# A planned attention and MLP kernel: instruction fetches in the planner's DMA model, and other splits of layer 1 in stripes 2 and 4

## The chip, the cores and the metric

The kernel runs on one core of a Trainium2 chip. The core has a matrix engine (PE, or TensorE), a vector engine (DVE), a scalar engine (ACT), a general engine (POOL, or GpSimd), and a synchronisation engine (SP) whose work here is to issue transfers. Sixteen DMA engines move data between HBM and the on-chip memory. Each engine works through its own instructions in order and waits on semaphores for the others. The metric is the device time of one execution in microseconds (us), lower is better. Durations of single instructions are in us or ns as the profile gives them.

## The reference

Two computations follow one another. The first is a decayed linear attention over 4 batches, 8 heads, 768 positions and head dimension 64, in blocks; the second is a two-layer MLP over the 3072 tokens that come out of it, with a piecewise quadratic activation.

```python
for b in range(nb):                      # blocks of 64 positions
    intra = einsum('bhic,bhjc->bhij', qb, kb) * Dmask
    intra = einsum('bhij,bhjd->bhid', intra, vb)
    inter = einsum('bhid,bhde->bhie', qb * lam_pow, kv_state)
    out[:, :, sl] = intra + inter
    kv_state = lam_block * kv_state + einsum('bhsd,bhse->bhde', kb_dec, vb)
x = out.transpose(0, 2, 1, 3).reshape(3072, 512)
h = x @ w_in                             # 512 -> 2048
g = where(h >= 1, h, where(h <= -1, 0, (h + 1) ** 2 / 4))
y = g @ w_out                            # 2048 -> 512
```

## The kernel before

The tokens are cut into 24 **chunks** of 128, six to a batch, and into six **stripes** of 512 tokens (four chunks each, stripes 0 to 5). Chunk c belongs to stripe c // 4.

*Attention, per chunk.* SP loads k and v of a chunk (256 KB each), and q for two chunks at a time (512 KB). GpSimd scales and casts q (line 249) and k (line 243; VectorE does k of the first four chunks). ScalarE casts v (line 263). From chunk 6 on, k and q are transposed by transfers that SP issues (lines 289 and 292); before that PE transposes them (lines 268 and 275). PE updates the running state ("u", line 298), which ScalarE copies out (line 302). PE forms the scores ("s", line 317 from chunk 4 on), VectorE masks them ("m", line 327), PE forms the chunk's output ("o", lines 334 and 337), and ScalarE casts that into the stripe's transposed activations xT ("x", line 344).

*MLP, per stripe.* Layer 1 is 16 steps, each of which fills one PSUM bank of 128 x 512 with h (line 365). With `PARTS[s] = n`, the stripe is cut into n parts of 512/n tokens: a step then computes n groups of 128 hidden features for one part, by 4n matmuls of 512/n columns, and a part's steps need only that part's chunks. Without an entry n is 1. ScalarE takes r = relu(h + 1) out of the bank (line 373). Two steps make one VectorE group: t (line 381), w (384) and gT (389). Layer 2 is 16 steps of four matmuls of 512 columns (line 408), four steps to each output tile of 128 tokens; ScalarE copies that out (line 413) and SP stores it (line 430). A layer-2 step of a stripe in several parts needs the groups of its part; in a stripe with n = 1 it needs the groups of its quarter of the features. PE works on layer 1 of stripe s and layer 2 of stripe s - 1 in turn, with attention of later chunks in between. The steps of layer 1 are counted through all stripes (16 for each, "step 32" is the first of stripe 2), and so are the groups (8 for each), the output tiles and their stores (4 for each).

*The order.* All of this is laid out ahead of time by a planner, `run_plan` (line 179), which runs while the program is built. `add` (line 175) registers an operation with its engine, an assumed duration, what it needs, and a due time. The planner simulates the engines with these assumed durations, and whenever an engine is free it takes, among the operations that are ready by then, the one with the earliest due time. It sends out the instructions of every engine in the order of the simulated start times. Transfers go through one modelled queue, `dma_free`: a transfer starts when the queue is free and occupies it for its `dma` time. On the chip each engine then keeps to this order, whatever arrives late.

Due times come from a ladder, `l_seq` (line 435): one step of `STEP` for each layer-1 and layer-2 step. An attention chunk is due (`o_due`, line 451) 3 us ahead of the first layer-1 step of the part that it belongs to, and chunks of the same part are 3 us apart. The transposes of q and k are due first of all on SP, then loads in their order, then stores.

Buffers also tie things together: six loads of k and of v and three of q may be in flight or unused, four cast k tiles, two banks for h, two for y, three VectorE groups, and eight output tiles that wait to be stored.

Of the kernel before, what the change touches and what calls it, by code (L numbers as in the profile page):

```python
# [23 lines left out]
def kernel(  # L24
# [24 lines left out]
    KO = d_model // 128  # L49
# [7 lines left out]
    LQ, NQ2 = 3, 3  # L57
# [4 lines left out]
    XT, NQT, NQK, RING = 6, 4, 4, 3  # L62
# [112 lines left out]
    def add(key, eng, ns, fn, needs=(), due=None, extra=0, dma=0, perf=False):  # L175
        OPS[key] = Op(key, eng, ns, fn, needs, due, extra, dma, perf)
        ops.append(OPS[key])

    def run_plan(free):

        users = {x.key: [] for x in ops}
        for x in ops:
            x.needs = [OPS[y] for y in x.keys if y in OPS]
            for y in x.needs:
                users[y.key].append(x)
        left = {x.key: len(x.needs) for x in ops}
        topo = [x for x in ops if not x.needs]
        for x in topo:
            for u in users[x.key]:
                left[u.key] -= 1  # L190
                if left[u.key] == 0:
                    topo.append(u)
        assert len(topo) == len(ops)
        for x in reversed(topo):
            d = [u.due - u.ns - x.extra - LAT for u in users[x.key] if not u.dma]
            x.due = min(d + ([x.own] if x.own is not None else []), default=1e9)
            if x.dma or x.key[0] in ("l1", "l2"):
                x.due = x.own
        left = {x.key: len(x.needs) for x in ops}
        ready = {e: [] for e in free}  # L200
        for x in topo:
            if not x.needs:
                ready[x.eng].append((0, x))
        out_seq, xfer, dma_free = [], [0] * RING, 0
        while len(out_seq) < len(ops):
            t, e = min((max(free[e], min(r for r, _ in lst), xfer[-RING] if e == "SP" else 0), e)
                       for e, lst in ready.items() if lst)
            r, x = min(((r, x) for r, x in ready[e] if r <= t), key=lambda p: (p[1].due, p[0]))
            ready[e].remove((r, x))
            ns = x.ns + (720 if x.perf and free["POOL"] > t else 0)  # L210
            free[e] = t + ns
            x.t, x.end = t, t + ns + x.extra
            if x.dma:
                dma_free = max(dma_free, t + (1300 if e == "SP" else 2100)) + x.dma
                x.end = dma_free + 1400
                if x.key[0] in ("ld", "lq") and x.key[1] >= (FAR if x.key[0] == "ld" else FAR // 2):
                    x.end += SLACK if (x.key[1] if x.key[0] == "ld" else 2 * x.key[1]) >= 10 else NEAR
                if e == "SP":
                    xfer.append(dma_free)
            out_seq.append((t, len(out_seq), x))  # L220
            for u in users[x.key]:
                left[u.key] -= 1
                if left[u.key] == 0:
                    ready[u.eng].append((max(y.t if y.eng == u.eng and y.key != u.gate else y.end + (XSL if u.eng == "SP" and y.eng == "POOL" and u.dma in (640, 1280) else LAT) for y in u.needs), u))
        for t, _, x in sorted(out_seq, key=lambda p: p[:2]):
            if DBG:
                print(f"{t / 1e3:9.3f} {x.due / 1e3:9.3f} {x.eng:5s} {x.ns:6.0f} {x.key}")
            x.fn()

    def mm(*cols):  # L230
        return sum(c / 2.4 + 3 for c in cols)


    qs, ks, kT, qT, sc_sb, xT, ptt, pst, pot = {}, {}, {}, {}, {}, {}, {}, {}, {}
# [56 lines left out]
    def f_qx(m):  # L291
        nc.sync.dma_start_transpose(out=qT_tile(m).rearrange("p e h j -> p (e h) j"), in_=qs[m].rearrange("p e h d -> p (e h d)"))
# [138 lines left out]


    T0, STEP, LEAD = 22000, 1057, 3000
    PARTS = {1: 4, 2: 4, 3: 2, 4: 2}
    l_seq = [(1, 0, i, 0) for i in range(FO)]
    for s in range(1, NST + 1):
        n = PARTS.get(s, 1)
        l1 = [(1, s, i, p) for p in range(n) for i in range(0, FO, n)]
# [44 lines left out]
    for it in order:  # L483
        if isinstance(it, tuple):
# [4 lines left out]
            if gated is not None:  # L489
                need.append(("w",) + w_seen[gated])  # L490
            add(("w",) + it, "POOL", 900, lambda it=it, wait=gated: f_w(it, wait), need, due=pos_ * 1e-3,
                dma=2560)
# [17 lines left out]
    for c in range(NCH):  # L510
        od, cb = o_due(c), c % NCB
        lastu = c - 1 if cb else c - 2
        m = c // 2
        e = "DVE" if c < CPS else "POOL"
        add(("cast", c, 1), e, 690 if e == "DVE" else 1060, lambda c=c, eng=(nc.vector if e == "DVE" else nc.gpsimd): cast(c, eng),
            [("ld", c, 1), ("cast", c - 1, 1), ("t", c - NQK), ("u", c - NQK)])
        add(("cast", c, 2), "ACT", 640, lambda c=c: cast_v(c),
            [("ld", c, 2), ("o", c - NV), ("u", c - NV), ("cast", c - 1, 2)])
        for i in range(2 if c % 2 == 0 else 0):
            old = ("tq", m - NQK // 2, i)  # L520
            add(("cq", m, i), "POOL", 1060, lambda m=m, i=i: cast_q(m, i, nc.gpsimd),
                [("lq", m), ("cq", m, 0) if i else None, old, ("qT",) + old[1:]])
            if m < XQ:
                add(("tq", m, i), "PE", mm(*[128] * 4), lambda m=m, i=i: f_tq(m, i),
                    [("cq", m, i)] + ([("kT", c - 1), ("m", c - 1, 1), ("tq", m, 0) if i else None] if c >= CPS else []),
                    due=od - 6000, extra=FILL)
                add(("qT", m, i), "ACT", 600, lambda m=m, i=i: f_qT(m, i), [("tq", m, i)])
            else:
                if i:
                    add(("qT", m, 1), "SP", 2000, lambda m=m: f_qx(m), [("cq", m, 1), ("o", 2 * (m - NQ2) + 1)], due=-2, dma=1280)  # L530
        if c < XT:
            add(("t", c), "PE", mm(*[128] * 4), lambda c=c: f_t(c),
                [("cast", c, 1), ("kT", c - 1), ("kb", c - 1, 0), ("kb", c - 1, 1), ("m", c - 1, 1) if c > 3 else None,
                 ("qT", m, 0) if c >= CPS and c % 2 == 0 and m < XQ else None, ("qT", m, 1) if c >= CPS and c % 2 == 0 and m < XQ else None],
                due=od - 6000, extra=FILL)
        else:
            add(("t", c), "SP", 1200, lambda c=c: f_kx(c), [("cast", c, 1), ("m", c - NQT, 1)], due=-2, dma=640)
        if CPS <= c < XT:
            add(("kT", c), "DVE", 450, lambda c=c: f_kT(c), [("t", c), ("m", c - NQT, 1)])
        for hi in range(2 if c < CPS else 0):  # L540
            add(("kb", c, hi), "DVE", 365, lambda c=c, hi=hi: f_kb(c, hi), [("t", c), ("s", c - NKB, 1)])
        if cb < NCB - 1:
            add(("u", c), "PE", mm(*[128] * 4), lambda c=c: f_u(c),
                [("cast", c, 1), ("cast", c, 2), ("ub", lastu, 0), ("ub", lastu, 1), ("u", lastu)], due=od - 4000, extra=FILL)
            for hi in range(2):
                add(("ub", c, hi), "ACT", 372, lambda c=c, hi=hi: f_ub(c, hi), [("u", c), ("o", c - NUB + 1)])
        if c >= CPS:
            add(("s", c, 0), "PE", mm(*[128] * 4) + 190, lambda c=c: f_s2(c),
                [("kT", c) if c < XT else ("t", c), ("qT", m, 0), ("qT", m, 1), ("m", c - 1, 0), ("m", c - 1, 1)], due=od - 2500, extra=FILL)
        for h in range(2):  # L550
            if c < CPS:
                add(("s", c, h), "PE", mm(*[128] * 4), lambda c=c, h=h: f_s(c, h),
                    [("kb", c, 0), ("kb", c, 1), ("qT", m, 0), ("qT", m, 1), ("m", c - 1, 0) if not h else ("t", c)], due=od - 3000 + 100 * h, extra=FILL)
            add(("m", c, h), "DVE", 690, lambda c=c, h=h: f_m(c, h), [("s", c, h if c < CPS else 0), ("o", c - 3), ("m", c, 0) if h else None])
        add(("o", c), "PE", mm(*[128] * (12 if cb else 8)), lambda c=c: f_o(c),
            [("m", c, 1), ("cast", c, 2), ("ub", c - 1, 0) if cb else None, ("ub", c - 1, 1) if cb else None,
             ("x", c - 1), ("o", c - 1)], due=od, extra=FILL)
        add(("x", c), "ACT", 600, lambda c=c: f_x(c), [("o", c), ("x", c - 1), ("l1", (c // CPS - 2) * FO - 1)])


    n1, last = 0, None
    l1_order = [x for x in l_seq if x[0] == 1]
    l2_order = [x for x in l_seq if x[0] == 2]
    NA = 4
# [4 lines left out]
    for n1, (_, s, i, p) in enumerate(l1_order):  # L569
# [2 lines left out]
        rw = RW  # L572
        j = (i // n) % rw
        grp = n1 // rw
        add(("l1", n1), "PE", mm(*[MS // n] * (KO * n)) if n1 >= NA else mm(*[C] * KO),
            lambda a=(s, i, n, p, 1 if n1 < NA else None): f_l1(*a),
            kx + [("w", 0, W_OF[i + n - 1]), ("la", n1) if n1 < NA else ("r", n1 - 2 if n1 >= NA + 2 else n1 - NA), ("l1", n1 - 1)], due=l_due[1, s, i, p], extra=FILL)
# [57 lines left out]
```

## Time and profile before

| what | us |
|---|---|
| median of 8 runs | 225.23 |
| lowest and highest of the 8 | 224.16, 228.63 |
| the profiled execution | 224.22 |
| its span, first to last instruction | 222.5 |
| layer 1 on PE (line 365), busy | 93.6 |
| layer 2 on PE (line 408), busy | 87.7 |
| VectorE, the three operations of a group, mean ns | 576, 806, 832 |
| ReLU on ScalarE, mean ns | 679 |
| VectorE idle ahead of its first group operation, waiting for the ReLU | 41.0 |
| GpSimd waiting for q loads, for k loads | 30.8, 17.6 |
| k transposed by a transfer, issue to landing, median (range) | 2.9 (2.4 to 5.3) |
| q transposed by a transfer, issue to landing, median (range) | 5.2 (3.3 to 6.7) |
| v load, issue to landing, median (range) | 5.4 (3.4 to 8.4) |

The granted TensorE clock was full in every slice of the span. In a row of the timeline the first number is the start in us from the start of the span, the second the length, then engine, line, operation, output and inputs, shape and count; what stands in brackets is how long the engine had stood idle before and what released it. PE overlaps the matmuls of a row, and the recorded length of one (219 ns for 128 columns) is longer than the distance to the next, so distances are taken from start to start. Some 30 matmul records are missing from the trace.

### The profile page before, as it was taken

What the parts mean: (1) busy time and instruction counts of PE and PEld (TensorE: products, weight loads), DVE (VectorE), ACT (ScalarE), POOL (GpSimd) and SP (SyncE); (2) the same over time, 40 slices, a digit from 0 to 9 for tenths busy, and PEclk for the clock granted to TensorE, in tenths of its full rate; (3) what the DMA queues carried; (4) which work ended last, traced back from release to release, by engine and by line L of the source; (5) the groups of instructions that cost most, each with busy time, mean ns of one, the idle gap of its engine ahead of it and who ended that gap; (6) DMA issues with size and microseconds to landing.
All of it is one profiled execution on the core that took longest, in us unless ns stands there. A gap on an engine that the chain in (4) does not pass through costs nothing. (4 is left out here: it accounts for less than half of the span.)

```text
span 222.5 us, 4630 instructions
## 1 busy us (share of the span) xinstructions
PE 204.2 (92%) x1874; PEld 135.2 (61%) x1904; DVE 144.2 (65%) x218; ACT 123.7 (56%) x221; POOL 64.6 (29%) x65
## 2 busy tenths in 40 slices
PE   0589897998999999999999989999999999999994
PEld 0376534776569787777667757767767644444442
DVE  4586496799656896989499458774556554654301
ACT  3475866546646866665665475767555445445030
POOL 7371074226625161918042065620000000000000
PEclk9999999999999999999999999999999999999999
DMA  5999999999997999979898999994011001110122
GB/s 130 240 201 199 188 242 200 183 227 216 172 259 150 191 200 203 170 173 185 197 183 313 239 216 270 194 210 98 2 47 50 20 27 50 47 47 0 47 97 94
DMA packets 89685, 34.39 MB, mean 155 GB/s; under 512 B 70080, under 2 KB 86720, under 8 KB 89664
## 3 DMA queue, kind: packets, MB, share of 16 engines
q1 hardware_dynamic: 85296, 29.89, 66.9%
q0 software_dynamic: 4224, 4.19, 11.9%
q8 instruction: 15, 0.25, 0.5%
q14 instruction: 6, 0.05, 0.1%
q10 hardware_dynamic: 144, 0.00, 0.0%
HBM read 27.27 MB, written 6.29 MB: 151 GB/s over the span
## 5 line engine op out<-in xcount | busy, mean ns | idle before, releaser
L365 PE MATMUL ph<-xT,w_in_sb 128*128 128x128 bf16 (+2 forms) x877 | 93.6, 255 | 0.9 <-ACT r L373 0.7
L373 ACT ACTIVATE r<-ph,one 128x512 bf16<-128x512 f32 (+2 forms) x96 | 64.6, 679 | 51.0 <-PE ph L365 35.6
L408 PE MATMUL py<-w_out_sb,gT 128*128 128x512 bf16 x341 | 87.7, 379 | 1.7 <-issue 0.5
L365 PEld LDWEIGHTS <-w_in_sb 128*128 128x128 bf16 x880 | 65.4, 98 | 24.3 <-issue 2.2
L381 DVE TENSOR_SCALAR t<-r 128x1024 bf16<-128x1024 bf16 x48 | 27.6, 576 | 41.0 <-ACT r L373 41.0
L408 PEld LDWEIGHTS <-gT 128*128 128x128 bf16 x368 | 33.9, 98 | 31.4
L389 DVE TENSOR_TENSOR gT<-w,t 128x1024 bf16<-128x1024 bf16 x48 | 39.9, 832 | 1.6
L249 POOL TENSOR_TENSOR qs<-x0f,tab_q 128x512 bf16<-128x512 f32 x24 | 28.8, 1220 | 38.3 <-DMA x0f<-in_q_dram 30.8
L384 DVE TENSOR_TENSOR w<-r,t 128x1024 bf16<-128x1024 bf16 x48 | 38.7, 806 | 1.3
L243 POOL TENSOR_TENSOR ks<-x1f,tab_k 128x512 bf16<-128x512 f32 x20 | 25.8, 1294 | 29.6 <-DMA x1f<-in_k_dram 17.6
L413 ACT COPY osb<-py 128x512 f32<-128x512 f32 x23 | 13.5, 586 | 14.4 <-PE py L408 12.7
L263 ACT CAST vi<-x2f 128x512 bf16<-128x512 f32 x24 | 14.9, 620 | 11.0 <-DMA x2f<-in_v_dram 10.9
L327 DVE TENSOR_TENSOR sc<-ps,causal 128x512 bf16<-128x512 f32 x20 | 13.8, 690 | 10.8 <-PE pt L317 10.8
L337 PE MATMUL po<-sc,vi 128*128 128x128 bf16 x192 | 18.2, 219 | 0.0
L344 ACT CAST xT<-po 128x512 bf16<-128x512 f32 x24 | 14.1, 588 | 6.8 <-PE po L337 3.0
L302 ACT CAST ubd<-pu 64x256 bf16<-64x256 f32 x40 | 14.6, 366 | 4.9 <-PE pu L298 4.5
L337 PEld LDWEIGHTS <-vi 128*128 128x128 bf16 x192 | 14.4, 98 | 2.7 <-issue 0.7
L334 PE MATMUL po<-qT,ubd 128*128 128x128 bf16 x80 | 14.5, 219 | 0.6 <-ACT xT L344 0.6
L327 DVE TENSOR_TENSOR sc<-pt,causal 128x512 bf16<-128x512 f32 x20 | 13.6, 681 | 0.0
L298 PE MATMUL pu<-vi,ks 128*128 128x128 bf16 x80 | 8.2, 228 | 1.8 <-POOL ks L243 1.1
L268 PE MATMUL pt<-ident,ks 128*128 128x128 bf16 x24 | 2.8, 249 | 7.3 <-DVE ks L243 7.2
L298 PEld LDWEIGHTS <-ks 128*128 128x128 bf16 x80 | 6.1, 102 | 4.5 <-POOL ks L243 2.2
(55 smaller groups left out, 89.0 us busy)
## 6 DMA issues: line engine op xcount, KB each, us to landing
x1f<-in_k_dram SPq DMA_DIRECT2D x24, 256.0 KB, 5.4
x0f<-in_q_dram SPq DMA_DIRECT2D x12, 512.0 KB, 5.6
x2f<-in_v_dram SPq DMA_DIRECT2D x24, 256.0 KB, 5.4
out_dram<-osb SPq DMA_DIRECT2D x23, 256.0 KB, 2.5
w_in_sb<-in_moe_w_in_dram POOLq DMA_DIRECT2D x4, 512.0 KB, 9.1
w_out_sb<-in_moe_w_out_dram POOLq DMA_DIRECT2D x4, 512.0 KB, 8.4
kT<-ks SPq DMA_TRANSPOSE x18, 2.9
out_dram<-osb SPq DMA_DIRECT2D x1, 192.0 KB, 1.9
```

The lines of the kernel that those rows point to most:

```text
L243: eng.tensor_tensor(ks[c], qkv_ld[c, 1], _bc(tab_k[:, c % NCB, :], 2, D), op=AX.mult)
L249: eng.tensor_tensor(qs[m, e], qkv_ld[m, 0][:, :, e], _bc(tab_q[:, e, m % (NCB // 2), :], 2, D), op=AX.mult)
L263: nc.scalar.copy(out=v_out(vi[c % NV]), in_=qkv_ld[c, 2].rearrange("p (a b) d -> p a b d", b=2))
L302: nc.scalar.copy(out=ubd[c % NUB][HD[hi], :, HD[hi]], in_=pu[0][HD[hi], :, HD[hi]])
L327: nc.vector.tensor_tensor(sc_sb[c][:, g], pst[c, g], _bc(causal, 1, HP), op=AX.mult)
L337: nc.tensor.matmul(po[:, hp], lhsT=vi[c % NV][:, hp, hi].rearrange("p a d -> p (a d)"), rhs=sc_sb[c][:, hi, hp, :], start=(cb == 0 and hi ...
L365: nc.tensor.matmul(ph[:, j * m:(j + 1) * m], lhsT=w_in_sb[:, ko, (ni + j) * 128:(ni + j + 1) * 128], rhs=xT[s][:, ko, part * m:(part + 1) ...
L373: nc.scalar.activation(out=r_t[grp][:, i, cs], in_=ph_t[s, ni, part][:, cs], func=AF.Relu, bias=one[:, 0:1])
L381: nc.vector.tensor_scalar(t_t[grp], r, 0.5, 1.0, op0=AX.mult, op1=AX.min)
L384: nc.vector.tensor_tensor(w_t[grp], r, t_t[grp], op=AX.subtract)
L389: nc.vector.tensor_tensor(gT[s][:, f - RW * n:f, part * m:(part + 1) * m], w_t[grp].rearrange("p a (b m) -> p (a b) m", m=m), t_t[grp].rea ...
L408: nc.tensor.matmul(py_t[s, ms], lhsT=gT[s][:, ko, ms * 128:(ms + 1) * 128], rhs=w_out_sb[:, ko, :], start=(ko == 0), stop=(ko == FO - 1))
```

## The change

There are three edits. First, the planner gets a model of PE's own instruction fetches. Every PE operation counts two instructions (a weight load and a matmul) for each of its matmuls: 8 matmuls for scores, 12 for a chunk's output, the layer-1 step's own number, 4 for everything else. Whenever the count passes a multiple of 256, the modelled DMA queue is taken for 1300 ns from that time on. Second, the assumed SP time of a q transpose goes from 2000 to 2450 ns. Third, stripe 2 is cut in two parts in place of four, and stripe 4 is left whole in place of two parts. No other line of the kernel is changed; the instructions of all operations but layer 1 of these two stripes stay as they were, and their order comes out of the planner.

```diff
+    MMS, FETCH = {"s": 8, "o": 12}, 1300
...
-        out_seq, xfer, dma_free = [], [0] * RING, 0
+        out_seq, xfer, dma_free, fetched = [], [0] * RING, 0, 0
...
             free[e] = t + ns
             x.t, x.end = t, t + ns + x.extra
+            if e == "PE":
+                n = fetched + 2 * MMS.get(x.key, MMS.get(x.key[0], 4))
+                if n // 256 > fetched // 256:
+                    dma_free = max(dma_free, t) + FETCH
+                fetched = n
             if x.dma:
                 dma_free = max(dma_free, t + (1300 if e == "SP" else 2100)) + x.dma
...
-    PARTS = {1: 4, 2: 4, 3: 2, 4: 2}
+    PARTS = {1: 4, 2: 2, 3: 2, 4: 1}
...
-                    add(("qT", m, 1), "SP", 2000, lambda m=m: f_qx(m), [("cq", m, 1), ("o", 2 * (m - NQ2) + 1)], due=-2, dma=1280)
+                    add(("qT", m, 1), "SP", 2450, lambda m=m: f_qx(m), [("cq", m, 1), ("o", 2 * (m - NQ2) + 1)], due=-2, dma=1280)
...
+        MMS["l1", n1] = KO * n if n1 >= NA else KO
         add(("l1", n1), "PE", mm(*[MS // n] * (KO * n)) if n1 >= NA else mm(*[C] * KO),
```

## The prediction

> **What bounds the kernel now.** I read the page first, for the engine that sets the end.
>
> ```profile
> span 222.5 us, 4630 instructions
> ...
> PE 204.2 (92%) x1874; PEld 135.2 (61%) x1904; DVE 144.2 (65%) x218; ACT 123.7 (56%) x221; POOL 64.6 (29%) x65
> ...
> DMA  5999999999997999979898999994011001110122
> ...
> q8 instruction: 15, 0.25, 0.5%
> ...
> PE 37%; DMA 2%; issue 1%; POOL 0%; DVE 0%; POOLq 0%
> ```
>
> TensorE is busy in 204.2 of 222.5 us, and the chain that ended last is nearly all PE, with one DMA in it. The DMA engines are full until about 145 us: attention loads decide when PE's attention pieces can run. All the change can win is PE's standing time and its pace; so I went through PE's timeline from matmul start to matmul start. From 7 to 25 us some 7 us are lost waiting on the prologue, whose order the change leaves alone. After 25 us PE really stands at four places, about 4 us together (a hole of 0.22 us beside a "x3" or "x7" of 512 columns is one missing record, not a wait):
>
> ```profile
> 34.39 0.40 PE L298 MATMUL pu<-vi,ks 128*128 128x128 bf16 x4 [1.05 <-POOL ks L243]
> ...
> 52.20 0.62 ACT L263 CAST vi<-x2f 128x512 bf16<-128x512 f32 x1 [2.79 <-DMA x2f<-in_v_dram]
> ...
> 52.87 0.38 PE L298 MATMUL pu<-vi,ks 128*128 128x128 bf16 x4 [0.57 <-ACT vi L263]
> ...
> 53.45 0.72 PE L365 MATMUL ph<-xT,w_in_sb 128*128 128x128 bf16 x10 [0.20 <-ACT r L373]
> ...
> 128.61 0.62 ACT L263 CAST vi<-x2f 128x512 bf16<-128x512 f32 x1 [2.39 <-DMA x2f<-in_v_dram]
> ...
> 129.87 1.03 PE L365 MATMUL ph<-xT,w_in_sb 128*128 128x256 bf16 x8 [0.52 <-ACT r L373]
> ...
> 144.17 3.63 DMA kT<-ks
> 147.80 0.05 issue
> ```
>
> Each time PE's fixed order asks for a chunk whose load, cast or transpose has not arrived. At 52 and 129 us ScalarE, itself in order, stands on a v load, and the ReLU that frees PE's bank is queued behind that cast.
>
> **The change, part by part.** The planner's new terms (a fetch charge, 2450 instead of 2000 for the q transpose) put no instruction into the program; they reorder it. The built program has 192 matmuls and 192 weight loads fewer, SP and POOL have the same instructions, and POOL the same order.
>
> *Pace.* Stripe 2 goes from 256 matmuls of 128 columns to 128 of 256, stripe 4 from 128 of 256 to 64 of 512. Starts of one 16-, one 8- and one 4-matmul step against the next:
>
> ```profile
> 89.58 1.06 PE L365 MATMUL ph<-xT,w_in_sb 128*128 128x128 bf16 x16
> 90.47 1.03 PE L408 MATMUL py<-w_out_sb,gT 128*128 128x512 bf16 x4
> 91.33 1.06 PE L365 MATMUL ph<-xT,w_in_sb 128*128 128x128 bf16 x16
> ...
> 112.63 1.04 PE L365 MATMUL ph<-xT,w_in_sb 128*128 128x256 bf16 x8
> 113.50 1.03 PE L408 MATMUL py<-w_out_sb,gT 128*128 128x512 bf16 x4
> ```
>
> A step of the same work takes 0.89, 0.87 and 0.86 us: 16 x 0.02 = 0.32 for stripe 2 and 16 x 0.01 (0.87 to 0.862 unrounded, 0.13) for stripe 4, **0.45 us** won. The Trainium skill, "TensorE: Matmul & The Clock Gate", Back-to-back issue gap, would make this the main thing: it gives about 81 ns sustained for a matmul of 128 columns with its weight load and 131 ns for 512 (98 ns for 256, by my interpolation). By that rule stripe 2 saves 256 x 81 - 128 x 98 = 8.2 us and stripe 4 128 x 98 - 64 x 131 = 4.2 us, an estimate of 12 us. The rows show 56, 109 and 216 ns at full granted clock, so weight loads are hidden already: I take 0.45.
>
> *The fetch charge.* The plan now stops its one model of the DMA queue for 1.3 us at every 256 PE instructions. The q8 row holds 15 fetches and 0.5% of 16 engines' span: 0.005 x 222.5 x 16 / 15 = 1.2 us each, but on one engine of 16. The skill ("Runtime: NRT & Kernel Launch", Instruction fetch mechanics) also says that crossing such a block is mostly hidden, which speaks against paying for it; in this trace no PE wait ends on one. By the rule the term is worth nothing; by the row it makes the plan up to 1.3 us too pessimistic about loads after each fetch. Its effect is only that attention is placed later behind its loads, which is what the waits above want.
>
> *Chunks 4 to 6.* PE's order was layer-1 step 10, q transpose, step 11, q transpose, then chunk 4; now one more step stands ahead of each transpose pair and of chunk 4's state update, 1.7 us of work. PE reaches that update at 34.5; its k cast ended at 34.34. The 1.2 us hole (33.12 to 34.39) and 0.3 us ahead of the transposes go; chunk 4's transpose then waits some 0.1 for ScalarE's copy out of its bank: **-1.4**. Chunk 6's update moves behind three more layer-2 steps (2.6 us): PE comes to it at about 53.3, its cast is done at 52.8. The holes there, 0.74 and 0.36 us, go; chunk 7's update may wait 0.1: **-1.0**.
>
> *Chunks 6 to 13.* Now I set PE's new turns (old starts, plus the steps moved ahead, less what was won) against landings. Chunk 6: turn 60.8, its transposes landed at 58.8 and 59.3 before and now sit ahead of a v load. Chunk 8: 73.1 against 70.4. Chunk 9: 76.9 against 75.8, now ahead of a v load. Chunk 10: 84.4; before, q and k landed at 85.2 and 85.9, but now they are issued ahead of both loads of chunk 13 (1.2 us of transfer each), so about 83.2: **the least slack, 1.2 us**. Chunk 11: 89.0 against some 86.4. Chunks 12 and 13: 3 us and more. Nothing added; the loads pushed back (v of chunk 8, k and v of 13, 15) are wanted by casts more than 3 us later.
>
> *Stripe 2 in halves.* Its first eight layer-1 steps now run with no layer-2 step between them. Two steps take PE 1.74 us and make one VectorE group, which takes 1.8 us alone and 4.1 us beside a GpSimd op:
>
> ```profile
> 37.44 0.42 DVE L381 TENSOR_SCALAR t<-r 128x1024 bf16<-128x1024 bf16 x1
> 37.89 0.69 DVE L384 TENSOR_TENSOR w<-r,t 128x1024 bf16<-128x1024 bf16 x1
> 38.62 0.69 DVE L389 TENSOR_TENSOR gT<-w,t 128x1024 bf16<-128x1024 bf16 x1
> ...
> 88.91 1.26 DVE L381 TENSOR_SCALAR t<-r 128x1024 bf16<-128x1024 bf16 x1
> 90.21 1.41 DVE L384 TENSOR_TENSOR w<-r,t 128x1024 bf16<-128x1024 bf16 x1
> 91.66 1.42 DVE L389 TENSOR_TENSOR gT<-w,t 128x1024 bf16<-128x1024 bf16 x1
> ```
>
> VectorE's order is chunk 10's mask, group 16, the first op of group 17, chunk 11's mask. The mask of 10 ends at about 86.3. With every op fast that of 11 ends by 90.1, before PE asks at 91.2; with every op slow (4.1 + 1.3 + 1.3) at 93.0, 1.8 late. GpSimd casts there about three quarters of the time, so not all are slow: I take **+0.65**, between 0 and 1.8. Behind it in PE's queue stand the chunk's output, xT and the second half. The first layer-2 step of stripe 2 now wants group 19 instead of 17: at about 105, against 99 to 106; 0, at most 1.3.
>
> *Chunks 16 to 23, stripe 4 whole.* Chunk 19's v cast moves on ScalarE from behind ReLU 55 to behind 61, some 8 us later than its load: the 0.69 us at 129 goes. All of chunk 19 must now precede stripe 4's first step. On SP, stores 9 and 10 move ahead of loads: store 9 (its copy ready near 122) ahead of chunk 19's, store 10 (near 131) ahead of those of 21 and 22 and of the k transpose of 19. From there I keep the old spacing (k load of 21 issued 130.3, transpose landed 142.0): it lands by 143.6, and PE asks at 146.4. Chunk 20's transposes wait on SP for store 11 (141) and land at 147; PE asks at 150.4 instead of 147.3: the 0.53 us goes. The eight steps of stripe 4 without layer 2 meet a GpSimd that is nearly done, so groups take 1.8 and cost nothing. From layer-1 step 71 on the two orders are the same.
>
> **Sum:** -0.45 - 1.4 - 1.0 + 0.65 - 0.69 - 0.53 = **-3.4 us**. The profiled execution goes from 224.2 (span 222.5) to 220.8. It is among the shorter of the eight runs (224.2 to 228.6); from their median, 225.2, the same step gives **221.8**.
>
> **Rivals.** *VectorE takes it back:* both bounds of the halves at their worst, 1.8 + 1.3, instead of 0.65: -1.0 or so, 224.3. For it: the slow rows above lie in that very stretch; against: between 89 and 105 us GpSimd was idle for 5.9 of 16. *The DMA queue is later than I place it (slower):* halves ask for chunks 9 and 11 up to four steps earlier, and everything is in one queue that is full. Lateness beyond 1.2 us at chunk 10 is paid one to one; from 5.7 us (1.2 + 3.4 + 1.1) the kernel is slower by the bound below, some 226.5 to 228. The q transposes' landing time ranges from 3.3 to 6.7 us: for it; but that spread alone costs 2.2 and leaves a gain. *Orders change, waits only move:* PE meets other casts late on ScalarE and the sum is near nothing, 225.
>
> **How the numbers follow.** Forecast 0.60 (own range 221.0 to 223.2); VectorE 0.10; waits only move 0.08; DMA late 0.22. Half a per cent, 1.1 us, is what can be told from no change. The first case is all faster, VectorE's half so: faster 0.64; same 0.14; slower 0.22. The range runs from 220.6 (all gains, no new wait, and half a microsecond of spread between runs) to 226.0, where the lighter part of the late DMA lies.
>
> **What would show it.** No PE wait near 34, 52 and 129 us; layer-1 steps of 0.87 in stripe 2; chunk 11's output matmuls behind a VectorE mask by about half a microsecond; chunk 19's turn not ended by a DMA. I am wrong if PE stands for 2 us or more in stripe 2, or ahead of stripe 4, on a transpose or a mask.

## The result, and the profile after

The kernel with the change takes 221.64 us (median of 11 runs, 221.35 to 222.30); the kernel before, in all its runs up to then, 224.88 us (32 runs, 222.60 to 228.63). The ratio, 0.9881 with a 95% interval from 0.9853 to 0.9908, compares the means of fast runs alone, 221.75 with 224.43 us, and leaves out the seven runs of before that took over 1.5% longer than its fastest. That is 1.2%, or 2.7 us. The prediction was 221.8.

The page after, in the rows that were shown of before:

```profile
span 220.0 us, 4245 instructions
...
PE 203.2 (92%) x1686; PEld 126.9 (58%) x1712; DVE 145.3 (66%) x218; ACT 123.8 (56%) x221; POOL 60.8 (28%) x65
...
DMA  5999999999898999799999698976501101110122
...
q8 instruction: 13, 0.21, 0.4%
...
PE 77%; DMA 15%; SPq 3%; POOL 2%; issue 1%; ACT 0%; DVE 0%
```

The busy shares hardly moved. The chain of waits did: before, it was lost among pieces that began at 130 us; now it can be followed through PE's unbroken work back to a single transfer, a part of the second weight, and from there into the prologue. Pieces of that chain (time, length, what):

```profile
35.78 8.51 DMA w_out_sb<-in_moe_w_out_dram
44.29 0.04 issue
44.33 0.38 PE py L415
```

And PE's timeline at the places where it still stands, with the scores of chunks 19 and 20, whose turns the prediction worked out (the line numbers are seven higher than in the kernel before):

```profile
34.07 0.38 PE L282 MATMUL pt<-ident,qs 128*128 128x128 bf16 x4 [0.17 <-ACT qT L288]
...
44.33 1.02 PE L415 MATMUL py<-w_out_sb,gT 128*128 128x512 bf16 x3 [0.49 <-DMA w_out_sb<-in_moe_w_out_dram]
...
89.65 0.92 PE L372 MATMUL ph<-xT,w_in_sb 128*128 128x256 bf16 x7 [0.57 <-ACT xT L351]
...
146.72 0.23 PE L324 MATMUL ps<-qT,kT 64*128 64x128 bf16 x1
...
150.64 0.23 PE L324 MATMUL ps<-qT,kT 64*128 64x128 bf16 x1
```

The holes near 34 (1.2 us), 52, 129 and 147 us are gone. The scores of chunks 19 and 20 start at 146.7 and 150.6 us with no wait in brackets; their transposes landed at 142.8 and 145.7. Three waits are new, measured from start to start: 0.33 us at 34 (the second q transpose waits for ScalarE's copy out of its bank), 0.66 us at 44 (layer 2 waits for the third quarter of its weights, landed at 44.29), and 0.73 us at 89 (a layer-1 step waits for the cast into xT).

The account starts where layer 1 runs in full width (25.1 us before, 25.4 after; ahead of it the profiled prologue took 0.3 us longer). Removed: 0.3 + 1.2, 0.74 + 0.36, 0.69 and 0.53, together 3.8 us, and 0.45 of pace; new: 1.7. That is -2.5; the stretch from there to the end is 2.8 us shorter (197.4 to 194.6), so 0.3 us of it has no place in this account.

### The profile page after: what moved, and what is told of

It reads as the page before. It is cut to its first block, busy times and chain, and to the rows that moved or that the text cites. A ratio compares the mean times of both kernels' runs of the same rounds, so it can differ in the third digit from the quotient of the medians.

```text
span 220.0 us, 4245 instructions
## 1 busy us (share of the span) xinstructions
PE 203.2 (92%) x1686; PEld 126.9 (58%) x1712; DVE 145.3 (66%) x218; ACT 123.8 (56%) x221; POOL 60.8 (28%) x65
## 4 chain that ended last, share of the span: by engine, by line
PE 77%; DMA 15%; SPq 3%; POOL 2%; issue 1%; ACT 0%; DVE 0%
PE py L415 35%; PE ph L372 31%; DMA w_out_sb<-in_moe_w_out_dram 7%; DMA w_in_sb<-in_moe_w_in_dram 5%; PE po L344 4%; PE ps L324 3%; DMA x0f<-in_q_dram 3%; SPq L476 2%; PE po L341 2%; PE pu L305 2%; PE py L409 1%; POOL w_in_sb L156 1%; POOL qs L256 1%; PE ph L409 0%; ACT xT L351 0%
## 5 line engine op out<-in xcount | busy, mean ns | idle before, releaser
L372 PE MATMUL ph<-xT,w_in_sb 128*128 128x128 bf16 (+2 forms) x682 | 91.1, 279 | 0.8 <-ACT xT L351 0.6
L415 PE MATMUL py<-w_out_sb,gT 128*128 128x512 bf16 x348 | 86.9, 379 | 1.8 <-DMA w_out_sb<-in_moe_w_out_dram 0.5
L372 PEld LDWEIGHTS <-w_in_sb 128*128 128x128 bf16 x688 | 55.8, 98 | 27.1 <-issue 1.4
L415 PEld LDWEIGHTS <-gT 128*128 128x128 bf16 x368 | 34.4, 98 | 35.4 <-issue 0.6
L396 DVE TENSOR_TENSOR gT<-w,t 128x1024 bf16<-128x1024 bf16 x48 | 38.1, 794 | 1.5
L250 POOL TENSOR_TENSOR ks<-x1f,tab_k 128x512 bf16<-128x512 f32 x20 | 22.4, 1122 | 43.4 <-DMA x1f<-in_k_dram 30.7
L341 PEld LDWEIGHTS <-ubd 128*128 128x128 bf16 x80 | 7.8, 98 | 1.4
```

What stands on the lines that cost most here:

```text
L250: eng.tensor_tensor(ks[c], qkv_ld[c, 1], _bc(tab_k[:, c % NCB, :], 2, D), op=AX.mult)
L341: nc.tensor.matmul(po[:, hp], lhsT=ubd[(c - 1) % NUB][:, hp, :], rhs=q_cols(c, hp), start=True, stop=False)
L372: nc.tensor.matmul(ph[:, j * m:(j + 1) * m], lhsT=w_in_sb[:, ko, (ni + j) * 128:(ni + j + 1) * 128], rhs=xT[s][:, ko, part * m:(part + 1) ...
L396: nc.vector.tensor_tensor(gT[s][:, f - RW * n:f, part * m:(part + 1) * m], w_t[grp].rearrange("p a (b m) -> p (a b) m", m=m), t_t[grp].rea ...
L415: nc.tensor.matmul(py_t[s, ms], lhsT=gT[s][:, ko, ms * 128:(ms + 1) * 128], rhs=w_out_sb[:, ko, :], start=(ko == 0), stop=(ko == FO - 1))
```

## The experiments

The theory: the gain comes from the **turns**, that is, from how many layer-1 and layer-2 steps stand ahead of each attention chunk on PE, and the planner's fetch charge alone moves these turns to where the data are. The rival: fewer and wider matmuls, and with them fewer fetches, made it. This table gives the steps ahead of the state update of chunk 6 and the scores of chunks 8, 9, 19 and 20 in each built program, with the measured ratio to before. Before's own median was 224.53, 224.11 and 223.84 us in the three later sets of runs, so runs of different sets are compared by their ratios and not by their times.

| kernel | 6 | 8 | 9 | 19 | 20 | ratio (95%) |
|---|---|---|---|---|---|---|
| before | 29 | 48 | 51 | 114 | 116 | 1 |
| after | 32 | 51 | 54 | 118 | 121 | 0.9881 (0.9853 to 0.9908) |
| PARTS alone | 29 | 45 | 48 | 109 | 116 | 1.0006 (0.9983 to 1.0029) |
| planner alone | 32 | 51 | 54 | 118 | 121 | 0.9887 (0.9847 to 0.9927) |
| fetch charge 0 | 29 | 45 | 48 | 109 | 116 | 1.0041 (1.0016 to 1.0066) |
| fetch charge 650 | 30 | 47 | 51 | 112 | 119 | 0.9939 (0.9918 to 0.9961) |
| fetch charge 2600 | 32 | 57 | 61 | 127 | 132 | 1.0163 (1.0128 to 1.0198) |
| 14% on all transfers | 32 | 50 | 54 | 118 | 124 | 0.9928 (0.9902 to 0.9953) |

**PARTS alone**, in the planner of before:

```diff
-    PARTS = {1: 4, 2: 4, 3: 2, 4: 2}
+    PARTS = {1: 4, 2: 2, 3: 2, 4: 1}
```

> Before's planner, after's PARTS. Order theory (the planner's later attention turns made the gain): no gain, since chunk 6's update again comes after 29 steps instead of 32, chunk 8 and 9 even three steps (2.6 us) earlier than before, so PE waits near 34, 52 and 75 us; 224.5 to 227, ratio 0.998 to 1.010. Width theory (fewer, wider matmuls and fewer fetches made it): about 222, ratio 0.988.

Measured: 224.59 us (22 runs), ratio 1.0006. The width theory falls: its 0.988 lies far outside the interval. PE's timeline of this run shows the waits that took back the pace, chunk by chunk (8, 9 and 19; the profiled execution took 226.09 us, longer than the median, so its waits may be too):

```profile
70.75 0.23 PE L317 MATMUL ps<-qT,kT 64*128 64x128 bf16 x1 [0.21 <-DMA kT<-ks]
...
76.12 0.23 PE L317 MATMUL ps<-qT,kT 64*128 64x128 bf16 x1 [1.17 <-DMA kT<-ks]
...
143.14 0.23 PE L317 MATMUL ps<-qT,kT 64*128 64x128 bf16 x1 [1.27 <-DMA kT<-ks]
```

With chunk 9 three steps earlier than before, PE stands for a transposed k that is still on its way.

**Planner alone**: after's kernel with PARTS of before.

> After's planner, before's PARTS. Order theory: most of the gain stays, no wait near 52 and 129 us, lost are 0.45 us of pace and won is the 0.7 us wait of the halves at 89 us: 221.4 to 222.6, ratio 0.986 to 0.992. Width theory: 224.5 to 225, ratio 0.998 to 1.

Measured: 221.68 us, ratio 0.9887, span 219.9: the whole gain, with 192 matmuls more than after. Its profile has no hole over 0.34 us after 25 us. The planner's edits change SP's order of loads, transposes and stores along with PE's turns; no run moves the turns alone.

**One stripe at a time**: after's kernel with `{1: 4, 2: 2, 3: 2, 4: 2}` and with `{1: 4, 2: 4, 3: 2, 4: 1}`.

> After with stripe 4 still in halves. Order theory: like after plus 0.13 us of pace: 221.5 to 222.1, ratio 0.988, with the wait near 89 us. Width theory: two thirds of the gain, 222.6, ratio 0.991.

> After with stripe 2 still in quarters. Order theory: 0.32 us of pace lost, the 0.7 us wait near 89 us gone: 221.0 to 222, ratio 0.984 to 0.989. Width theory: one third of the gain, 223.8, ratio 0.996.

Measured: 222.46 (ratio 0.9915, 0.9883 to 0.9947) with stripe 2 in halves, and 221.59 (0.9895, 0.9857 to 0.9932) with stripe 4 whole. The first median is above what was expected, and its interval begins at the order theory's number and holds the width theory's, so it tells nothing on the split. The second excludes the width theory's 0.996. The profile of the first has the wait at 88 us (0.73 us) again and that of the second has none there: halves of stripe 2 win 0.3 us of pace and cost 0.7 in a wait.

**After's order, before's widths.** The plan is untouched; a step of stripes 2 and 4 is issued in half as many columns at a time.

```diff
+        sub = 2 if s in (2, 4) else 1
         for j in range(n):
-            for ko in range(KO):
+            for h in range(sub):
+                for ko in range(KO):
```

> After's plan and order, but layer 1 of stripes 2 and 4 is issued in the widths of before (128 and 256 columns): 192 matmuls and weight loads more, two more fetches. By the rows of before it costs 0.45 us against after (222.1, ratio 0.990); by the page's sustained figures 12 us (234); if nothing hides in the order, nothing.

Measured: 222.21 us, ratio 0.9917 (0.9890 to 0.9945): by the ratios 0.8 us above after, with intervals that overlap, and nowhere near 12. It is no clean measure of the 0.45 us of the rows, since the waits changed along with the widths: after's wait at 89 us did not come (more on this below), and another did. The timelines of VectorE with one row of GpSimd, then of PE, in this run:

```profile
87.58 1.42 DVE L394 TENSOR_TENSOR w<-r,t 128x1024 bf16<-128x1024 bf16 x1
89.03 1.42 DVE L399 TENSOR_TENSOR gT<-w,t 128x1024 bf16<-128x1024 bf16 x1
90.37 1.26 DVE L391 TENSOR_SCALAR t<-r 128x1024 bf16<-128x1024 bf16 x1
91.55 0.68 DVE L334 TENSOR_TENSOR sc<-ps,causal 128x512 bf16<-128x512 f32 x1
...
88.41 2.94 POOL L256 TENSOR_TENSOR qs<-x0f,tab_q 128x512 bf16<-128x512 f32 x2
```

```profile
91.52 0.22 PE L341 MATMUL po<-qT,ubd 128*128 128x128 bf16 x1
92.28 0.22 PE L344 MATMUL po<-sc,vi 128*128 128x128 bf16 x1 [0.54 <-DVE sc L334]
92.88 0.22 PE L344 MATMUL po<-sc,vi 128*128 128x128 bf16 x1 [0.38 <-DVE sc L334]
```

Here group 16 and the first operation of group 17 all ran beside GpSimd's casts, which went on without a break from 86.2 to 92.5 us, and chunk 11's output stood 1.25 us for its mask. In after GpSimd stood idle from 86.9 to 88.4 us, and group 16 (86.8 to 88.7) fell into that gap:

```profile
86.82 0.42 DVE L388 TENSOR_SCALAR t<-r 128x1024 bf16<-128x1024 bf16 x1
87.27 0.69 DVE L391 TENSOR_TENSOR w<-r,t 128x1024 bf16<-128x1024 bf16 x1
88.00 0.69 DVE L396 TENSOR_TENSOR gT<-w,t 128x1024 bf16<-128x1024 bf16 x1
88.61 1.27 DVE L388 TENSOR_SCALAR t<-r 128x1024 bf16<-128x1024 bf16 x1
90.94 0.69 DVE L334 TENSOR_TENSOR sc<-ps,causal 128x512 bf16<-128x512 f32 x1 [1.06 <-PE pt L324]
...
88.42 2.35 POOL L256 TENSOR_TENSOR qs<-x0f,tab_q 128x512 bf16<-128x512 f32 x2 [1.52 <-DMA x0f<-in_q_dram]
```

The bracket of the last VectorE row says that VectorE waited for PE, not PE for VectorE.

**Is it the fetch model, or just lateness?** Four runs. First the charge at zero, half and double (`FETCH = 0`, `650`, `2600`):

> After with the fetch charge at 0, so that of the planner's edits only the 2450 ns of the q transpose is left. If the fetch term alone moves the turns: as the run with after's PARTS alone, waits near 34, 52, 75 and 142 us, 224 to 225, ratio 0.997 to 1.003. If the 2450 ns do part of it: 222.5 to 223.5.

> Fetch charge halved to 650 ns. Chunk 6's update comes after 30 steps (before 29, after 32), chunk 9 after 51 (51, 54), chunk 19 after 112 (114, 118). If each microsecond of lateness pays until the data are there: about half the gain, 222.5 to 223.5, with some of the waits near 52, 75 and 142 us left. If any charge will do: 221.6.

> Fetch charge doubled to 2600 ns. If later is only slack: as after, 221.3 to 222.3. If turns can be too late: chunk 19 now comes after 127 steps instead of 118 and 20 after 132 instead of 121, layer 2 of stripe 3 is used up before layer 1 of stripe 4 begins, and PE runs at VectorE's and ScalarE's pace there: 223 to 226.

Measured: 224.18, 222.58 and 227.68 us. At zero the turns are again those of PARTS alone, and the waits near 34, 53 and 76 us are back; the one near 143 is not in this profile. The 2450 ns do nothing that can be seen here; with the charge on they were not tried apart. PE in that run, at chunks 4 and 9:

```profile
34.77 0.40 PE L305 MATMUL pu<-vi,ks 128*128 128x128 bf16 x4 [1.05 <-POOL ks L250]
...
75.89 0.23 PE L324 MATMUL ps<-qT,kT 64*128 64x128 bf16 x1 [1.69 <-DMA kT<-ks]
```

At 650 about half of the gain is there (0.6% of 1.2%). At 2600 attention comes too late, and the loss is larger than expected (227.68, not 223 to 226). PE waits on the other engines instead: 63 of the 64 layer-2 steps of stripes 0 to 3 stand ahead of chunk 19, so only one is left to fill in, and in stripe 4 PE stands for xT and for VectorE's masks (for a mask of stripe 2 too, 1.4 us at 99 us). Two of these places, in PE's timeline of that run:

```profile
160.58 1.89 PE L372 MATMUL ph<-xT,w_in_sb 128*128 128x512 bf16 x7 [0.80 <-ACT xT L351]
...
182.14 0.22 PE L344 MATMUL po<-sc,vi 128*128 128x128 bf16 x1 [0.62 <-DVE sc L334]
```

Then no fetches, but every modelled transfer 14% longer, which is about the same 19 us of queue time in all:

```diff
-                    dma_free = max(dma_free, t) + FETCH
+                    pass
...
-                dma_free = max(dma_free, t + (1300 if e == "SP" else 2100)) + x.dma
+                dma_free = max(dma_free, t + (1300 if e == "SP" else 2100)) + 1.14 * x.dma
```

> No fetch term; instead every modelled transfer takes 14% longer, about the same 19 us of queue time in all (15 x 1.3), spread evenly. If only the later turns matter: within 0.5 us of after, 221.3 to 222.3, ratio 0.986 to 0.990. If the moments of the fetches matter: 223 or more.

Measured: 222.34 us, ratio 0.9928 (0.9902 to 0.9953), just outside what lateness alone was given and well short of what the rival was. The big waits are gone here too; others came, in PE's timeline at 34 us (0.84 us from start to start) and 81 us (0.85 us for one mask):

```profile
34.06 0.38 PE L282 MATMUL pt<-ident,qs 128*128 128x128 bf16 x4 [0.67 <-ACT qT L288]
...
81.65 0.22 PE L344 MATMUL po<-sc,vi 128*128 128x128 bf16 x1 [0.38 <-DVE sc L334]
```

About 0.6 of the gain is lateness alone. Whether the fetches' moments make the rest is not shown: the two plans also differ in where smaller waits fall.

**The wait at 89 us.** Only the second matmul of the step waits. In the instruction list of after, the step's first two matmuls both carry a wait on ScalarE:

```
Matmult ph_1440<-xT_1280,w_in_sb_160 128x256 [waits Activation_49]
Ldweights w_in_sb_160
Matmult ph_1440<-xT_1280,w_in_sb_160 128x256 [waits Activation_49]
```

The first wait is for a ReLU, the second for the cast of chunk 10 into xT. xT holds four rows of 512 tokens for each partition. The cast writes tokens 256 to 383 of all four rows; as one span that reaches from 256 to 1919. The step reads tokens 0 to 255 of each row: its first matmul lies outside that span, its second (512 to 767) inside it, though no element is shared. The cast in turn waits for PE to be done with the step before, which shares no element with it either. So the theory was that the program's waits are set by spans. The kernel with xT by chunk:

```diff
-            xT[sx] = xp.tile([128, KO, MS], BF16, name="xT", tag="xT")
-        nc.scalar.copy(out=xT[sx][:, :, off:off + C].rearrange("p h (j e) -> p h j e", e=2),
+            xT[sx] = xp.tile([128, CPS, KO, C], BF16, name="xT", tag="xT")
+        nc.scalar.copy(out=xT[sx][:, off // C].rearrange("p h (j e) -> p h j e", e=2),
...
-                                 rhs=xT[s][:, ko, part * m:(part + 1) * m],
+                                 rhs=xT[s][:, part * m // C:(part + 1) * m // C, ko],
```

> After with xT laid out by chunk (128 x chunk x 4 x 128) so that a chunk's write and the read of other chunks no longer overlap as spans. The theory that the 0.73 us wait near 89 us (second matmul of a step behind the cast of chunk 10) and the 0.67 us near 22 us (behind chunk 3) come from that: both waits go, 220.2 to 221.2, ratio 0.981 to 0.985. Rival, that a bank waits on the ReLU: nothing changes, 221.7.

Measured: 221.06 us, ratio 0.9874 (0.9841 to 0.9906; 0.981 to 0.985 was expected), span 218.8. The second wait is gone from the list and both holes from PE's timeline; at 22 us, after and then this kernel:

```profile
22.37 0.33 PE L365 MATMUL py<-xT,w_in_sb 128*128 128x384 bf16 x1
23.21 0.97 PE L365 MATMUL py<-xT,w_in_sb 128*128 128x384 bf16 x5 [0.51 <-ACT xT L351]
```

```profile
22.76 0.98 PE L365 MATMUL py<-xT,w_in_sb 128*128 128x384 bf16 x5
```

That the layout brings these waits is shown; the step from 221.64 to 221.06 is not, since the two intervals overlap. And spans are not the whole rule. In the built program of after's order in before's widths, the second matmul of the same step reads 512 to 639, inside the same span, and carries no wait for the cast, and the cast none for the step before. ScalarE's cast of chunk 10 in after and then in that run:

```profile
89.01 0.59 ACT L351 CAST xT<-po 128x512 bf16<-128x512 f32 x1 [0.58 <-PE ph L372]
```

```profile
87.88 0.58 ACT L351 CAST xT<-po 128x512 bf16<-128x512 f32 x1
```

So reads of 256 columns were tied to the cast and reads of 128 were not; by what rule stays open.

Two more on top of it, with stripe 2 in quarters, and with the second weight's landing set 1.5 us later in the plan (`x.end` of the `("w", 1)` loads) against the wait at 44 us:

> The run with xT by chunk, with stripe 2 in quarters again. If halves cost only the wait that the layout has removed: 0.3 us slower than that run by the pace, 221.0 to 221.6, ratio 0.986 to 0.990. If halves still cost something at VectorE: faster, 220.3 to 220.9.

> The run with xT by chunk, and the planner told that the second weight's loads land 1.5 us later, so that the third layer-2 quarter comes later and PE does not wait near 43.5 us for its load. If that wait is all that changes: 0.4 us less, 220.4 to 220.9, ratio 0.983 to 0.986. If it only moves (chunk 6 comes after 30 steps again): 221 to 222.

Measured: 221.78 (0.9899, 0.9845 to 0.9952) and 221.67 us (0.9893, 0.9848 to 0.9938); neither is better than xT by chunk, and the first lies above both ranges that were expected. In it the wait at 43 us was 0.76 us and one of 0.54 us for a mask came at 136, so it doesn't separate the pace from the halves' cost. (In one and the same PE order, that of after, the wait at 43 us was 0.66 us in after and 0.41 in xT by chunk: one profile is one sample of such a race.) In the second the wait only moved; its PE timeline has no hole at 44 us but these:

```profile
36.35 1.02 PE L372 MATMUL ph<-xT,w_in_sb 128*128 128x512 bf16 x4 [0.81 <-ACT r L380]
...
49.45 0.22 PE L344 MATMUL po<-sc,vi 128*128 128x128 bf16 x1 [0.38 <-DVE sc L334]
```

## Why the prediction was right

- **Pace, -0.45**: right by the rows. In after, too, matmuls of 128, 256 and 512 columns start 56, 109 and 216 ns apart. The 12 us that the sustained figures of the Trainium skill ("TensorE: Matmul & The Clock Gate", Back-to-back issue gap) would give are out: undoing the widths cost 0.6 to 0.8 us. That this is near 0.45 is in part luck, since the waits changed too.
- **The fetch charge**: right that it places attention later, and that this is what the waits wanted; the zero, half and double charges show it. That it stands for fetches is not needed: spreading the same lateness over all transfers brings about 0.6 of the gain (0.72% of 1.19%).
- **Chunks 4 to 6, -2.4**: the old holes went as said. Mis-sized was the new wait for ScalarE's copy, 0.33 in place of 0.1, and it came one step earlier, at the second q transpose. Missed was another: layer 2 comes forward here and meets the third quarter of its weights, 0.66 us. The step looked at attention's data and not at the weights' landing; before, that quarter landed at 44.23 and the first layer-2 step that needs it started at 47.09, 2.8 us later than now:

```profile
47.09 1.03 PE L408 MATMUL py<-w_out_sb,gT 128*128 128x512 bf16 x3
```

- **Chunks 6 to 13, nothing**: right. The slack at chunk 10 was larger than said: its k landed at 80.5, not 83.2, and PE came at 85.2. The least was at chunk 9, 3.4 us (74.4 against 77.8).
- **Stripe 2 in halves, +0.65**: the size was right by luck, the mechanism wrong in after: 0.73 us, but at the cast into xT, which waits and is waited for across elements that it does not share. The prediction put that at nothing. The predicted one, the mask behind a VectorE group slowed by GpSimd, came in the run with before's widths (1.25 us, within the 0 to 1.8).
- **Chunks 16 to 23, -1.2**: right. PE asked for chunks 19 and 20 at 146.7 and 150.6 (146.4 and 150.4 predicted), and both holes went.
- The sum was -3.4; the profiles give -2.5 in the span and -2.8 behind the prologue, and the ratio 1.2%, which is 2.7 us. The two waits that were missed or mis-sized, 0.9 us together, make up the difference. That 221.8 came so near 221.64 is luck: it starts from 225.2, the median of eight runs, which lies 0.8 us above the 224.4 of the ratio, and this offsets a step that was 0.7 us too large. For the profiled execution the prediction was 220.8, and it took 221.67. Of the rivals, waits that only move came in part: 1.7 us of new waits against 3.8 removed. VectorE took nothing back in after, only in other runs, and late transposes held PE up only in kernels with earlier turns than after's.

## What to carry to other kernels

In a kernel whose one engine follows a fixed order, count the steps ahead of each piece that depends on a transfer, and compare its turn with the landing time; in these runs, being a few steps early cost the whole wait, and being late cost nothing until work to stand in front of it ran out. A planner's queue model can be worth tuning on that ground alone; of the four values tried the best lies between two losses (0, 650, 1300 and 2600 ns gave 1.004, 0.994, 0.988 and 1.016 of the time before). When work moves forward, look at every input that it needs, weights too. Where a matmul in the middle of a group waits, see whether the program carries a wait between a write and a read that share no element, and whether another layout of the buffer removes it.

## What had not been expected

The spread between runs shrank with the waits: the eight first runs of before lie between 224.2 and 228.6 us, the eleven of after between 221.35 and 222.30. The kernels with the old turns spread likewise (PARTS alone: 223.8 to 230.0 in 22 runs). Why was not tried. A matmul whose moving operand comes as two or four pieces of 128 columns (xT by chunk) showed no loss of pace: in that kernel as in after, matmuls of 256 and 512 columns start 109 and 216 ns apart.
